# Spreading three tiles, a late norm and a shorter opening in a linear-attention and MLP kernel on one core

## The chip, the cores and the metric

The kernel runs on one core of one Trainium2 chip. The metric is the time of one execution on the device in microseconds (us), the median of several runs. TensorE (PE in the profile; PEld is its weight loads) makes the matrix products, VectorE (DVE), ScalarE (ACT) and GpSimd (POOL) work on their results, SyncE (SP) issues transfers.

## The reference, cut to what matters

```python
kv  = einsum('bhsd,bhse->bhde', k, v)          # 8 batches, 8 heads, 576 rows, 64 columns
out = einsum('bhsd,bhde->bhse', q, kv)
out = out / sqrt(mean(out*out, -1) + 1e-6) * g_norm
x   = out as 4608 tokens x 512                 # heads side by side
h   = x @ w_in                                 # 512 x 2048
g   = max(h, 0) + alpha * min(h, 0)
y   = g @ w_out                                # 2048 x 512
```

The inputs are f32, products are made in f16 and summed in f32.

## The kernel before

The 4608 tokens are worked in nine blocks of 512. A block has 16 units. A unit is one group of four h products (`w_in`, 128 of the 2048 columns), its relu on ScalarE and its `gt` on VectorE; TensorE fills the rest of the unit with y products of finished `gt`s.

```python
def m1_evac(h_ps, w, g):                       # after the four h products of unit g
    nc.scalar.activation(out=m_sb, in_=h_ps, func=Relu, scale=-1.0)
    nc.vector.scalar_tensor_tensor(out=gt, in0=m_sb, scalar=beta[g], in1=h_ps, ...)
```

Attention comes in two forms. Batches 0 and 1 are made with columns of x in PSUM: `step_ot` (product and square), `ssq_mm` (a product that sums squares over a head, then Ln and Exp on ScalarE), `norm` (VectorE). The last 128 columns of batch 1, the "tail", belong to block 2 and go the same way. Batches 2 to 7 are made in tiles of 128 rows, spread over units of the block before: `tile_a` (product, square on ScalarE), `tile_b` (reduce on VectorE), `tile_c` (Ln, Exp, and `rg` on GpSimd), `tile_d` (the row on VectorE, and a transpose by DMA into `xm`, the block's x). Block 2's x is the tail and the first three tiles of batch 2, which are made in block 1.

```python
def tile_d(b, t):
    nc.vector.tensor_mul(out=x, in0=ot_ps, in1=rg)
    nc.sync.dma_start_transpose(out=xm(w)[:, :, c:c+m], in_=x)      # xm(w): all 512 columns of block w

lags = (0, 1, 3) if w == NB_PE else (0, 1, 2)                       # units between a, b+c and d
...
step_tail_ot(0, O1)                  # ahead of block 1
...                                  # in block 1, after unit 1 and unit 3:
            if (w, g) == (1, 1): step_tail_ssq(0, (ps_o, "o0"))
            if (w, g) == (1, 3): tail_norm(0)
            if (w, g) == (1, 2):     # gate: q and k of batch 3 load after q of batch 2 is transposed
                nc.gpsimd.tensor_copy(out=gate, in_=qtms[2][0:1, 0, 0:1]); load(3, "q"); load(3, "k")
            if (w, g) == (1, 11):    # gate: v of batch 3 loads after block 2's x has landed
                nc.gpsimd.tensor_copy(out=gate, in_=xm(2)[0:1, 0, W-1:W]); load(3, "v")
```

A load of q, k or v is two transfers, 320 and 256 KB. The opening (batches 0 and 1) has idle products, `keep_warm(n)`, that are meant to keep the TensorE clock up; block 0's y products fill TensorE while batch 1's attention is made, from about 32 to 50 us.

Of the kernel before, what the change touches and what calls it, by code (L numbers as in the profile page):

```python
# [17 lines left out]
def kernel(  # L18
# [11 lines left out]
    nc = tc.nc  # L30
# [9 lines left out]
    TPW = W // P  # L40
# [4 lines left out]
    NF = D_FF // P  # L45
# [3 lines left out]
    NB_PE = 2  # L49
# [35 lines left out]
    stages, bufs = [], []  # L85
# [4 lines left out]
    def zero_rest(st):  # L90
        nc.vector.memset(st[REM:P, :, TPP, :], 0.0)
# [30 lines left out]
        for nm in ("q", "k"):  # L122
            regroup(b, nm, eng=nc.gpsimd)

    for st in stages:
        for nm in "qkv":
            zero_rest(st[nm])

    ident = const_p.tile([P, P], FP32, name="ident")
    make_identity(nc, ident[:])  # L130
# [17 lines left out]
    nc.vector.memset(eps_t[:], 1e-6)  # L148
    ident16 = const_p.tile([P, P], FP16, name="ident16")
    nc.vector.tensor_copy(out=ident16[:], in_=ident[:])  # L150

    g2col = const_p.tile([P, 1], FP32, name="g2col")
    nc.sync.dma_start(out=g2col[0:64, :], in_=g_norm[:].unsqueeze(1))
# [48 lines left out]
    def keep_warm(n):  # L202
        for i in range(n):
            nc.tensor.matmul(  # L204
                out=warm_ps[:], lhsT=mask16[:], rhs=warm16[:], start=True, stop=True,
            )
# [84 lines left out]
    def ssq_mm(w, j, pool=(ps_o, "o2")):  # L291
        ot_ps, sq = ots.pop((w, j))
        ssq_ps = pool[0].tile([P, W], FP32, name="ssq_ps", tag=pool[1])
        nc.tensor.matmul(out=ssq_ps[:], lhsT=mask16[:], rhs=sq[:], start=True, stop=True)
        rstd = attn_p.tile([P, W], FP32, name="rstd")
        nc.scalar.activation(  # L296
            out=rstd[:], in_=ssq_ps[:], func=AF.Ln, bias=eps_t[:], scale=inv_d,
        )
        nc.scalar.activation(out=rstd[:], in_=rstd[:], func=AF.Exp, bias=0.0, scale=-0.5)  # L299
        ots[w, j] = (ot_ps, rstd)  # L300
# [12 lines left out]
    def half_ot(i, pool, eng=None):  # L313
        ot_ps = pool[0].tile([P, 2, HW], FP32, name="ot_ps", tag=pool[1])
        for u in range(2):
            nc.tensor.matmul(
                out=ot_ps[:, u, :], lhsT=kvs[0, 2 + u],
                rhs=qts[0, 2 + u][:, i * HW : (i + 1) * HW], start=True, stop=True,
            )
        sq = attn_p.tile([P, 2, HW], FP16, name="sq_sb", bufs=4)  # L320
        square(sq, ot_ps, [P, 2, HW], eng)
        ots["half", i] = (ot_ps, sq)
# [23 lines left out]
    def step_tail_ot(i, pool):  # L346
        ot_ps = pool[0].tile([P, JT, TAIL], FP32, name="ot_ps", tag=pool[1])
        for u in range(JT):
            j = i * JT + u
            nc.tensor.matmul(  # L350
                out=ot_ps[:, u, :], lhsT=kvs[NB_PE - 1, j],
                rhs=qts[NB_PE - 1, j][:, S - TAIL : S], start=True, stop=True,
            )
        sq = attn_p.tile([P, JT, TAIL], FP16, name="sq_sb", bufs=4)
        nc.scalar.activation(out=sq[:], in_=ot_ps[:], func=AF.Square)
        ots["tail", i] = (ot_ps, sq)

    def step_tail_ssq(i, pool):
        ot_ps, sq = ots.pop(("tail", i))
        ssq_ps = pool[0].tile([P, JT, TAIL], FP32, name="ssq_ps", tag=pool[1])  # L360
        nc.tensor.matmul(out=ssq_ps[:], lhsT=mask16[:], rhs=sq[:], start=True, stop=True)
        rstd = attn_p.tile([P, JT, TAIL], FP32, name="rstd")
        nc.scalar.activation(
            out=rstd[:], in_=ssq_ps[:], func=AF.Ln, bias=eps_t[:], scale=inv_d,
        )
        nc.scalar.activation(out=rstd[:], in_=rstd[:], func=AF.Exp, bias=0.0, scale=-0.5)
        ots["tail", i] = (ot_ps, rstd)

    def tail_norm(i):
        ot_ps, rstd = ots.pop(("tail", i))  # L370
        nc.vector.scalar_tensor_tensor(
            out=xm(NB_PE)[:, i * JT : (i + 1) * JT, 0:TAIL], in0=ot_ps[:], scalar=g2col[:],
            in1=rstd[:], op0=ALU.mult, op1=ALU.mult,
        )
# [18 lines left out]
    def next_o():  # L393
        n_tile[0] += 1
        return ps_o, f"o{(n_tile[0] - 1) % 3}"
# [48 lines left out]
    def phase_steps(w):  # L444


        if w >= NW:
            return []
        todo = [(b, t) for b in range(NB_PE, min(B, w + 1)) for t in range(NT)
                if (b, t) not in done and b * S + t * P < (w + 1) * W]  # L450
        done.update(todo)
        steps = []

        kv_at = {NB_PE: 3, NB_PE + 1: 6, NB_PE + 2: 2}.get(w, 0)
        n = {NB_PE: 4, NB_PE + 1: 2}.get(w, 0)
        steps += [([], [], []) for i in range(n)]

        lags = (0, 1, 3) if w == NB_PE else (0, 1, 2)
        if w in (NB_PE + 1, NB_PE + 2):
            k = [b for b, t in todo].index(w)  # L460
            todo[k:k] = [None] * (3 if w == NB_PE + 1 else 1)
        for i in range(len(todo) + lags[2]):
            a, b, d = (
                [todo[i - k]] if 0 <= i - k < len(todo) and todo[i - k] else [] for k in lags
            )
            begin = [lambda x=x: tile_b(*x) for x in b] + [lambda x=x: tile_d(*x) for x in d]
            mid = [lambda x=x: tile_c(*x) for x in b]
            end = [lambda x=x: tile_a(*x) for x in a]
            steps.append((begin, mid, end))
        if w < B:  # L470
            steps[kv_at][2 if w == NB_PE else 1].append(lambda: step_kv(w, pool=next_o() if kv_at else (ps_s, "s")))
        return steps
# [91 lines left out]
    )  # L564
    spread_g()
    load_rest()
    keep_warm(4)
    step_kv(0, 0, 2)
    keep_warm(2)
    step_ot(0, 0)  # L570
# [8 lines left out]
    load_batch(2)  # L579
    half_ot(0, (ps_s, "s"))  # L580
    norm(0, 1)
    half_ot(1, (ps_y, "y"), nc.vector)
    first = [ps_h.tile([P, W], FP32, name="h_ps", tag=f"h{g}") for g in range(3)]
    first += [ps_o.tile([P, W], FP32, name="h_ps", tag=f"o{g}") for g in range(2)]
    m1_mm(first[0], 0, 0, (0,))
# [34 lines left out]
    def ahead(g0, g1, tiles=range(TPW)):  # L620
        for g in range(g0, g1):
            for a in tiles:
                y_mm(ys[a], 0, a, g)

    S_POOL = (ps_s, "s")
    O1 = (ps_o, "o1")
# [12 lines left out]
    step_ot(1, 0, H_POOL[0])  # L639
    step_ot(1, 1, O1)  # L640
    step_ot(1, 2, H_POOL[1], nc.vector)
    ahead(8, 9)
    ssq_mm(1, 0, S_POOL)
    ahead(9, 10)
    ssq_mm(1, 1, S_POOL)
    norm(1, 0)
# [10 lines left out]
    y_out(ys[0], 0, 0)  # L657
    ahead(QW, NF, (1,))
    norm(1, 3)
    step_tail_ot(0, O1)  # L660
    ahead(QW, NF, (2,))
    y_out(ys[1], 0, 1, nc.vector)
    y_out(ys[2], 0, 2)
# [8 lines left out]
    AHEAD = NF - 2  # L672
    for w in range(1, NW):
        steps = phase_steps(w + 1)
        for g in range(NF):
            if g == LOAD_G and 4 < w + 2 < B:
                load_batch(w + 2)
            if w == 1:
                parts = [(0, g - NF + AHEAD)] if g >= NF - AHEAD else []
            else:  # L680
                n0 = AHEAD if w == 2 else 0
                n1 = TPW * NF - n0
                parts = [divmod(n0 + i, NF) for i in range(n1 * g // NF, n1 * (g + 1) // NF)]
            begin, mid, end = steps.pop(0) if steps else ([], [], [])
            for f in begin:
                f()
            m1_group(w, g, [H_POOL[1], S_POOL, H_POOL[2], H_POOL[0]][g % 4] if w == 1 else None)
            for f in mid:
                f()
            for a, gg in parts:  # L690
                if gg == 0:
                    pool, tag = ((ps_y, "y"), (ps_s, "s"))[a % 2]
                    y = pool.tile([P, W], FP32, name="y_ps", tag=tag)
                wy = w if w == 1 else w - 1
                y_mm(y, wy, a, gg)
                if gg == NF - 1:
                    y_out(y, wy, a)
            if (w, g) == (1, 1):
                step_tail_ssq(0, (ps_o, "o0"))
            if (w, g) == (1, 3):  # L700
                tail_norm(0)
            for f in end:
                f()
            if (w, g) == (1, 0):
                regroup(2, "k", eng=nc.gpsimd)
            if (w, g) == (1, 2):


                gate = const_p.tile([1, 1], FP16, name="gate")
                nc.gpsimd.tensor_copy(out=gate[:], in_=qtms[2][0:1, 0, 0:1])  # L710
                load(3, "q")
                load(3, "k")
            if (w, g) == (1, 8):
                regroup(3, "q", eng=nc.gpsimd)
            if (w, g) == (1, 11):

                nc.gpsimd.tensor_copy(out=gate[:], in_=xm(2)[0:1, 0, W - 1 : W])
                load(3, "v")
                transpose_q(3)
                regroup(3, "k", eng=nc.gpsimd)  # L720
            for i in {5: (0, 1), 6: (2, 3), 7: (4,), 8: (5,)}.get(g, ()) if w == 2 else ():
                load_part(4, "qkv"[i // 2], i % 2 == 0)
            if w > 1 and g == LOAD_G + 3 + 3 * (w == 2) and w + 2 < B:
                regroup_batch(w + 2)
            if w > 1 and g == NF - 3 and w + 2 < B:
                transpose_q(w + 2)
# [43 lines left out]
```

## Time and profile before

| | before |
|---|---|
| median, range of 4 runs | 293.52 us, 293.33 to 294.04 |
| span of the profiled run | 291.4 us |
| TensorE busy | 96% |
| time between TensorE starts beyond the columns' own time | 7.95 us |
| of it before 21.2 us / 21.2 to 73 us / after | 5.06 / 2.86 / 0.03 |
| first product of blocks 1, 2, 3 | 50.14, 70.89, 98.10 us |

The fourth row counts, for each product, the time to the start of the next less columns/2.4 + 2.5 ns (216 ns for 512 columns). Such time ahead of one product is called a hole below.

### The profile page before, as it was taken

What the parts mean: (1) busy time and instruction counts of PE and PEld (TensorE: products, weight loads), DVE (VectorE), ACT (ScalarE), POOL (GpSimd) and SP (SyncE); (2) the same over time, 40 slices, a digit from 0 to 9 for tenths busy, and PEclk for the clock granted to TensorE, in tenths of its full rate; (3) what the DMA queues carried; (4) which work ended last, traced back from release to release, by engine and by line L of the source; (5) the groups of instructions that cost most, each with busy time, mean ns of one, the idle gap of its engine ahead of it and who ended that gap; (6) DMA issues with size and microseconds to landing.
All of it is one profiled execution on the core that took longest, in us unless ns stands there. A gap on an engine that the chain in (4) does not pass through costs nothing.

```text
span 291.4 us, 4273 instructions
## 1 busy us (share of the span) xinstructions
PE 280.4 (96%) x1547; PEld 137.0 (47%) x1547; DVE 167.5 (57%) x258; ACT 153.6 (53%) x299; POOL 99.1 (34%) x109
## 2 busy tenths in 40 slices
PE   4999999999999999999999999999999999999994
PEld 1444464444454454454445544554445444444443
DVE  4469745687668576448744764488448644444300
ACT  1379349675657565438644754476448544444210
POOL 8822421565358228424733373233003100000000
PEclk9999999999999999999999999999999999999999
DMA  7999999999699916991699179844212311222133
GB/s 91 198 206 205 198 205 198 190 218 148 115 119 213 193 30 107 209 198 31 106 207 205 34 122 207 167 49 90 46 36 56 81 36 41 47 48 47 37 74 72
DMA packets 66197, 35.54 MB, mean 122 GB/s; under 512 B 32753, under 2 KB 61697, under 8 KB 66177
## 3 DMA queue, kind: packets, MB, share of 16 engines
q0 software_dynamic: 29632, 18.35, 45.0%
q1 hardware_dynamic: 36384, 16.80, 28.3%
q8 instruction: 12, 0.20, 0.3%
q10 hardware_dynamic: 160, 0.13, 0.2%
q14 instruction: 9, 0.07, 0.1%
HBM read 36.71 MB, written 9.44 MB: 158 GB/s over the span
## 4 chain that ended last, share of the span: by engine, by line
PE 88%; ACT 3%; DVE 3%; DMA 2%; issue 1%; POOL 1%; DVEq 0%; POOLq 0%
PE h_ps L482 40%; PE y_ps L509 38%; PE kv_ps L245 3%; PE otm_ps L401 2%; DMA qst<-in_q_dram 2%; DVE gt L491 1%; PE yb L509 1%; PE yc L509 1%; PE ya L509 1%; PE yd L509 1%; PE qt_ps L221 1%; ACT m_sb L489 1%; ACT rstd L296 1%; PE ot_ps L278 1%; ACT rstd L299 1%
## 5 line engine op out<-in xcount | busy, mean ns | idle before, releaser
L491 DVE SCALAR_TENSOR_TENSOR gt<-m_sb,beta_sb,h_ps 128x512 f16<-128x512 f32 x144 | 105.6, 744 | 75.8 <-ACT m_sb L489 75.5
L509 PE MATMUL y_ps<-w_out_sb,gt 128*128 128x512 f16 (+1 forms) x528 | 131.3, 373 | 0.8 <-DVE gt L491 0.8
L489 ACT ACTIVATE m_sb<-h_ps 128x512 f32<-128x512 f32 x144 | 85.4, 597 | 85.8 <-PE h_ps L482 84.0
L482 PE MATMUL h_ps<-xm,w_in_sb 128*128 128x512 f16 x448 | 115.0, 379 | 0.0
L509 PEld LDWEIGHTS <-gt 128*128 128x128 f16 x592 | 57.5, 98 | 66.8 <-DVE gt L491 2.7
L482 PEld LDWEIGHTS <-w_in_sb 128*128 128x128 f16 x584 | 55.6, 98 | 60.5 <-issue 1.0
L425 POOL TENSOR_TENSOR rg<-ss,g_all 128x512 f32<-128x512 f32 (+1 forms) x30 | 31.2, 1041 | 80.5 <-ACT ss L423 75.7
L482 PE MATMUL h_ps<-xt,w_in_sb 128*128 128x512 f16 (+1 forms) x136 | 30.8, 366 | 0.5 <-DMA w_in_sb<-in_moe_w_in_dram 0.3
L519 ACT COPY y_sb<-y_ps 128x512 f32<-128x512 f32 (+1 forms) x32 | 18.4, 576 | 15.6 <-PE y_ps L509 15.3
L413 DVE TENSOR_REDUCE ss<-sqm_sb 128x8 f32<-128x512 f32 (+1 forms) x30 | 20.5, 683 | 9.6 <-ACT sqm_sb L407 9.4
L434 DVE TENSOR_TENSOR xrow<-otm_ps,rg 128x512 f16<-128x512 f32 (+1 forms) x30 | 20.5, 682 | 3.6 <-POOL rg L425 3.6
L407 ACT ACTIVATE sqm_sb<-otm_ps 128x512 f32<-128x512 f32 (+1 forms) x30 | 17.7, 590 | 7.2 <-PE otm_ps L401 7.2
L112 POOL COPY ksb<-kst 128x2560 f16<-128x2560 f16 x6 | 13.9, 2324 | 15.7 <-DMA kst<-in_k_dram 15.7
L112 POOL COPY qsb<-qst 128x2560 f16<-128x2560 f16 x5 | 11.6, 2316 | 8.5 <-issue 8.5
L401 PEld LDWEIGHTS <-qtm 128*128 128x128 f16 x120 | 9.2, 98 | 7.9 <-issue 1.1
L401 PE MATMUL otm_ps<-kv_sb,qtm 128*128 128x128 f16 x120 | 11.6, 219 | 0.6 <-DVE kv_sb L249 0.6
L204 PE MATMUL warm_ps<-warm,mask 128*128 128x512 f16 x21 | 7.3, 489 | 4.1 <-DVE eps_t L148 4.1
L245 PEld LDWEIGHTS <-ksb 128*128 128x128 f16 x160 | 9.6, 98 | 2.5 <-issue 0.8
L420 ACT ACTIVATE ss<-ss,eps_t 128x8 f32<-128x8 f32 (+1 forms) x30 | 9.0, 301 | 2.8 <-DVE ss L413 2.6
L245 PE MATMUL kv_ps<-vst,ksb 128*128 128x128 f16 x160 | 10.4, 219 | 0.0
L231 ACT COPY qt_sb<-qt_ps 128x576 f16<-128x576 f16 x4 | 2.4, 638 | 12.4 <-PE qt_ps L221 12.4
L249 DVE TENSOR_TENSOR kv_sb<-kv_ps,mask 128x512 f16<-128x512 f32 (+1 forms) x9 | 5.6, 625 | 5.2 <-PE kv_ps L245 5.2
(76 smaller groups left out, 129.5 us busy)
## 6 DMA issues: line engine op xcount, KB each, us to landing
out_dram<-y_sb SPq DMA_DIRECT2D x70, 128.0 KB, 2.4
qst<-in_q_dram POOLq DMA_DIRECT2D x8, 320.0 KB, 4.8
kst<-in_k_dram POOLq DMA_DIRECT2D x7, 320.0 KB, 8.7
vst<-in_v_dram POOLq DMA_DIRECT2D x7, 320.0 KB, 10.5
qst<-in_q_dram POOLq DMA_DIRECT2D x8, 256.0 KB, 6.3
w_in_sb<-in_moe_w_in_dram POOLq DMA_DIRECT2D x4, 512.0 KB, 10.1
w_out_sb<-in_moe_w_out_dram POOLq DMA_DIRECT2D x4, 512.0 KB, 14.4
kst<-in_k_dram POOLq DMA_DIRECT2D x7, 256.0 KB, 9.5
```

The costliest lines, as they stand in the source:

```text
L112: (eng or nc.vector).tensor_copy(out=bufs[b % NBUF][nm][:, :, h0:h1, :].rearrange("p t h d -> p h t d"), in_=stages[b % NBUF][nm][:, h0:h1],)
L245: nc.tensor.matmul(out=kv_ps[:, j - j0, :], lhsT=ks(t), rhs=vs(t), start=(t == 0), stop=(t == NT - 1),)
L401: nc.tensor.matmul(out=ot_ps[:, 2 * j : 2 * j + 2, :], lhsT=qtms[b][:, t * NPAIR + j, :], rhs=kvs[b, j], start=True, stop=True,)
L407: nc.scalar.activation(out=sq[0:n], in_=ot_ps[0:n], func=AF.Square)
L413: nc.vector.tensor_reduce(out=ss[0:n], in_=sq[0:n], op=ALU.add, axis=mybir.AxisListType.X,)
L425: nc.gpsimd.tensor_tensor(out=rg[0:n], in0=ss[0:n].unsqueeze(2).to_broadcast([n, H, D]), in1=g_all[0:n].unsqueeze(1).to_broadcast([n, H, D ...
L434: nc.vector.tensor_mul(out=x[0:n], in0=ot_ps[0:n], in1=rg[0:n])
L482: nc.tensor.matmul(out=h_ps[:, cols], lhsT=w_in_blk(c, g), rhs=xt_of(w, c)[:, cols], start=(c == 0), stop=(c == NC - 1 and cols.stop == W),)
L489: nc.scalar.activation(out=m_sb[:], in_=h_ps[:], func=AF.Relu, scale=-1.0)
L491: nc.vector.scalar_tensor_tensor(out=gt[:], in0=m_sb[:], scalar=beta_sb[:, g : g + 1], in1=h_ps[:], op0=ALU.mult, op1=ALU.add,)
L509: nc.tensor.matmul(out=y[:], lhsT=gts[w, g][:, a * P : (a + 1) * P], rhs=w_out_blk(g)[:, cols], start=(g == 0), stop=(g == NF - 1),)
L519: nc.scalar.copy(out=y_sb[:, cols], in_=y[:])
```

## The change

Its intent: in block 1, keep VectorE and ScalarE from getting more work in a few units than they can finish; free a bank earlier for the fourth `ot`; start TensorE's useful work sooner.

```diff
 opening
-    for st in stages:                          # memsets of both buffers first
-        for nm in "qkv": zero_rest(st[nm])
+    for nm in "qkv": zero_rest(stages[0][nm])   # the other buffer's come after the constants
...
-    keep_warm(4)
+    keep_warm(2)
...
-    half_ot(1, (ps_y, "y"), nc.vector)          # square by copy and product on VectorE
+    half_ot(1, (ps_y, "y"))                     # square on ScalarE

 batch 1
-    ahead(8, 9)
+    ahead(8, 9, range(2))
     ssq_mm(1, 0, S_POOL)
+    ahead(8, 9, range(2, TPW))
...
-    step_tail_ot(0, O1)

 block 1
-        lags = (0, 1, 3) if w == NB_PE else (0, 1, 2)
+        lags = (0, 1, 4) if w == NB_PE else (0, 1, 2)
+        if w == NB_PE:
+            todo = [x for t in todo for x in (t, None)][:-1]     # a tile every second unit
...
-            if (w, g) == (1, 1): step_tail_ssq(0, (ps_o, "o0"))
-            if (w, g) == (1, 3): tail_norm(0)
+            if (w, g) == (1, 9): step_tail_ot(0, next_o())
+            if (w, g) == (1, 11): step_tail_ssq(0, next_o())
+            if (w, g) == (1, 13): tail_norm(0)
...  (the two pieces of batch 3's work on GpSimd: after unit 9 and 12 instead of 8 and 11)

 block 2: y products per unit
-                parts = [... for i in range(n1 * g // NF, n1 * (g + 1) // NF)]
+                n1, d = TPW * NF - n0, 2 * (w == 2)                # one in the first unit, not three
+                cut = lambda i: max(0, (n1 + d) * i // NF - d)
+                parts = [... for i in range(cut(g), cut(g + 1))]
```

More of the change, by code (lines that the diff above doesn't have):

```diff
@@ L123, in regroup_batch @@
             regroup(b, nm, eng=nc.gpsimd)
-    for st in stages:
-        for nm in "qkv":
-            zero_rest(st[nm])
+    for nm in "qkv":
+        zero_rest(stages[0][nm])
     ident = const_p.tile([P, P], FP32, name="ident")
@@ L150 @@
     nc.vector.tensor_copy(out=ident16[:], in_=ident[:])
+    for nm in "qkv":
+        zero_rest(stages[1][nm])
     g2col = const_p.tile([P, 1], FP32, name="g2col")
@@ L681 @@
                 n0 = AHEAD if w == 2 else 0
-                n1 = TPW * NF - n0
-                parts = [divmod(n0 + i, NF) for i in range(n1 * g // NF, n1 * (g + 1) // NF)]
+                n1, d = TPW * NF - n0, 2 * (w == 2)
+                cut = lambda i: max(0, (n1 + d) * i // NF - d)
+                parts = [divmod(n0 + i, NF) for i in range(cut(g), cut(g + 1))]
             begin, mid, end = steps.pop(0) if steps else ([], [], [])
@@ L697 @@
                     y_out(y, wy, a)
-            if (w, g) == (1, 1):
-                step_tail_ssq(0, (ps_o, "o0"))
-            if (w, g) == (1, 3):
-                tail_norm(0)
             for f in end:
                 f()
+            if (w, g) == (1, 9):
+                step_tail_ot(0, next_o())
+            if (w, g) == (1, 11):
+                step_tail_ssq(0, next_o())
+            if (w, g) == (1, 13):
+                tail_norm(0)
             if (w, g) == (1, 0):
@@ L712 @@
                 load(3, "k")
-            if (w, g) == (1, 8):
+            if (w, g) == (1, 9):
                 regroup(3, "q", eng=nc.gpsimd)
-            if (w, g) == (1, 11):
+            if (w, g) == (1, 12):
                 nc.gpsimd.tensor_copy(out=gate[:], in_=xm(2)[0:1, 0, W - 1 : W])
```

## The prediction

> **What bounds the kernel now.** I read the page first (busy shares, the row of DMA), then the waits of the two TensorE rows, then the chain in order of time for 50 to 73 us, and at each place where TensorE stood still the timeline and the landing of the transfer concerned.
>
> ```profile
> PE 280.4 (96%) x1547; PEld 137.0 (47%) x1547; DVE 167.5 (57%) x258; ACT 153.6 (53%) x299; POOL 99.1 (34%) x109
> DMA  7999999999699916991699179844212311222133
> ```
>
> TensorE is the bound. Its spans overlap (512 columns are shown as 379 ns, yet successive products start 216 ns apart), so I count time lost as start to next start less 216 ns (56 ns for 128 columns). By that count 7.9 us of the 291.4 are lost, all before 73 us: 4.8 before 21 us, the rest in few holes. The transfer row is full until about 45 us. From 73 us on products follow each other without a hole, so time saved earlier counts one for one, unless a transfer then comes late.
>
> The holes of block 1 (the second 512 tokens, 50.1 to 70.9 us), in the chain in order of time:
>
> ```profile
> 54.42 1.41 DVE gt L491 x2
> 55.83 0.66 DVE xm L371
> 56.49 0.61 DVE kv_sb L249
> 57.09 0.14 issue
> 57.23 0.38 PE otm_ps L401 x4
> ...
> 62.45 0.67 DVE xrow L434
> 63.12 0.67 DVE gt L491
> 63.79 0.05 issue
> 63.84 0.39 PE y_ps L509
> ```
>
> Twice the chain leaves TensorE for VectorE. The masked kv stands behind xm (the late norm of batch 1's last columns): the product before started at 56.22, so 57.23 - 56.22 - 0.216 = 0.79 us are lost. Then three tiles in successive units pile up reduces and rows ahead of gt: 0.76 before 63.84, and by the same count 0.165 each before 65.09 and 66.34. The weight row names the same releaser, and kv_sb's as "issue":
>
> ```profile
> PEld L509 <- DVE gt L491: 2.7, 4, 1.1
> PEld L401 <- issue: 1.1, 1, 1.1
> PEld L278 <- DVE xt L305: 0.7, 1, 0.7
> ```
>
> Before block 1 the fourth ot waits for a bank that batch 1's first norm frees; the start of block 2 waits for the last gt:
>
> ```profile
> 44.35 0.38 PE L509 MATMUL yd<-w_out_sb,gt 128*128 128x512 f16 x1
> 44.94 0.39 PE L278 MATMUL ot_ps<-qt_sb,kv_sb 128*128 128x64 f16 x2 [0.21 <-DVE xt L305]
> ...
> 71.75 0.38 PE L509 MATMUL y_ps<-w_out_sb,gt 128*128 128x512 f16 x1
> 72.31 0.60 PE L509 MATMUL y_ps<-w_out_sb,gt 128*128 128x512 f16 x2 [0.18 <-DVE gt L491]
> ```
>
> These are 0.375 and 0.34 us; 0.08 more lies ahead of the ssq at 43.49. Last, where the opening ends for good: the kv of batch 1, and the last part of v that it needs.
>
> ```profile
> 38.48 0.38 PE L509 MATMUL yd<-w_out_sb,gt 128*128 128x512 f16 x1
> 38.77 1.28 PE L245 MATMUL kv_ps<-vst,ksb 128*128 128x128 f16 x20
> ```
>
> The second fence is the view of one tile, narrowed to that transfer's issue: when it was issued, and how long it took to land.
>
> ```profile
> L102 POOL DMA_DIRECT2D vst<-in_v_dram x1: 677/677/677, 25.4 to 25.4; - x1
> DMA to landing us min/median/max: 13.2/13.2/13.2
> ```
>
> 25.4 + 13.2 = 38.6: kv started as soon as v had landed, with TensorE 0.07 us early. This decides what the opening is worth.
>
> **What the Trainium skill says.** "TensorE: Matmul & The Clock Gate", section "Back-to-back issue gap": N/2.4 + 2.5 ns warm, 216 ns for 512 columns; the starts in this trace agree, so 379 ns spans must not be summed. "PSUM — Partial Sum Buffer", section "Engine vs sequencer instructions": VectorE and ScalarE run strictly in order; the trace agrees (kv_sb behind xm above), so moving an instruction in a queue is the whole effect of this change. "DMA: Bandwidth & Descriptors", section "Issuing engines are not separate DMA queues": all share 16 engines; the trace agrees: the transpose of a row issued at 63.15 took 4.8 us to land under batch 3's loads, the one at 66.40 took 2.5 after them.
>
> **The change part by part.**
>
> 1. Opening. Two idle products go (2 x 0.216 = 0.43 us); three memsets of 0.27 us move behind the constants, so warm-up starts 0.8 us earlier, which nothing waits for (q lands at 7.8 us either way). The second half's square moves from VectorE (0.68 + 0.69, ready at 18.76) to ScalarE (0.58, ready about 17.3 by my estimate). But the first slice of w_in lands at 9.0 + 7.5 = 16.5, when the first h product starts now, and the second at 18.98, against 19.05 for its first user. What can go is mainly the 0.34 us hole at 20.6 to 21.2. And then q of batch 1 (landed 35.5, regrouped to 36.41; its transposes start 36.71) and v (38.6) hold TensorE: of anything gained, 0.07 survives. **-0.07.**
>
> 2. ssq of batch 1 two products earlier. ssq 41.90 instead of 42.33, then Ln 0.69, Exp 0.63, norm 0.75 with their gaps follow 0.43 earlier: the norm ends at 44.45 instead of 44.88. The fourth ot needs it at 44.57. Both holes close: **-0.45.**
>
> 3. Tail and tiles in block 1. The tail's four products and ssq (0.22 + 0.22) move into the block, no work is added. I laid out the block by hand, zero at its first product: a unit is 4 x 0.216 = 0.86, from unit 2 on plus one y of 0.216; kv 1.12 after unit 3, tiles 0.22 after 4, 6, 8, tail 0.22 after 9, ssq after 11. ScalarE starts a relu 0.20 after the last product's slot; relu 0.60; gt 0.74; reduce and row 0.69 and 0.68, about 0.07 less apiece back to back. kv ends at 5.00, kv_sb is then first in line and done at 5.88; the first tile starts at 6.08: the 0.79 is gone. gt 4 to 9 end at 7.44, 8.75, 9.90, 11.17, 12.45, 13.73, and the y that need them come at 8.25, 9.55, 10.63, 11.94, 13.24, 14.32: two units of spacing leave 0.6 us or more. The tight end is where the tail's Ln and Exp (1.35 us) hold relu 12 until 16.4: gt 12 ends at 17.78, wanted at 17.78; the tail norm ends at 19.14, wanted by block 2 at 19.13. The third row ends at 16.70, and its transpose with 2.5 us of landing comes at 19.25. So I leave 0.25 us of waiting, of 1.88 lost now: **-1.63.**
>
> 4. Block 2 takes one y instead of three in its first unit: the last y of the first 128 tokens comes 1.08 us later than its gt needs. **-0.34.**
>
> Block 3's first product now waits 0.03 us, counted as gone. Sum: 0.07 + 0.45 + 1.63 + 0.34 + 0.03 = 2.52; 293.48 - 2.52 = 290.96. I add 0.15 because every error in so tight a layout adds a wait: **291.1 us.**
>
> **Rivals.**
> (a) The opening's 0.43 to 0.6 us counts in full: about 290.5. For it: TensorE is the bound on average. Against: the 38.6 landing.
> (b) Block 2 starts on a transfer: the last transpose takes 4.8 us, not 2.5, because batch 3's loads are still in flight. They landed by 67.4; I put the issue at 66.2 of the new run (block 1 starts at 50.14 - 0.07 - 0.45 - 0.22 = 49.4). That costs up to 1 us: 292.
> (c) VectorE still falls behind near the tail, whose norm and ssq now meet the third tile: a wait takes the place of the one removed, 0.5 to 1 us: 291.6 to 292.
> (d) Block 3 gives it all back. Its columns' last transpose landed at 98.05 and its first product started at 98.10: no slack at all. If batch 4's loads (issued 81.0 to 88.6, landed by 96.3) did not move, all gain of parts 2 to 4 would be a wait there: 293.4. Against: GpSimd issues them behind its own work for block 2's tiles, so they follow TensorE's progress. I give this one in ten.
> (e) The warm-up ends at about 7.5, 0.9 us before the transposes, and the clock could rise later; the opening's slack before 38.6 would hide it.
>
> **Range and chances.** All holes after 38 us sum to 2.75, so without (a) the floor is 290.7, with its last 0.4 us about 290.3. (b) and (c) set the upper side at 292.3; (d) lies beyond and is most of the chance left out. Two per cent is 5.9 us, more than twice all holes after 38 us together, and nothing is added to TensorE: faster 0.01, within 2% 0.98, slower 0.01.
>
> **What would show it.** Right: the hole before batch 1's kv, or before its q transposes, grows from 0.07 to about 0.4 us in sum and kv stays at 38.7; no hole at ot (44.5); the waits of TensorE's weight row for gt fall from 2.7 us to below 0.7 and the 1.1 for kv_sb vanishes; block 2's first product moves from 70.9 to about 68.7, and block 3's from 98.1 to about 95.6. Wrong: kv of batch 1 well before 38.6 (a), a wait for xm at the start of block 2 (b) or block 3 (d), or holes on gt around units 10 to 14 (c).

## More of the kernel before

The lines that carry the reading are shown in the prediction. Two more serve as a measure for later: the two stretches from the first product of block 1 to that of block 2, and on to that of block 3. Columns: stretch, its length, and busy time (and instructions) of PE, PEld, DVE, ACT, POOL, then the granted clock, the DMA share and GB/s.

```profile
50.14:70.89 20.75, 19.52 (x113) 9.21 (x111) 15.58 (x24) 13.28 (x29) 10.98 (x12) 1.00 1.18 191
70.89:98.10 27.21, 27.03 (x155) 13.23 (x154) 18.93 (x29) 16.76 (x35) 16.86 (x16) 1.00 1.01 151
```

VectorE is busy 15.6 of 20.75 us in block 1, so it has time enough. What it lacks is the right order.

## The result

| | before | changed |
|---|---|---|
| median | 293.52 us | 291.50 us |
| range of 4 runs each | 293.33 to 294.04 | 291.14 to 291.92 |
| span of the profiled run | 291.4 us | 289.9 us |
| first product of blocks 1, 2, 3 | 50.14, 70.89, 98.10 | 49.59, 69.77, 96.60 |

The ratio is 0.9929, with a 95% interval of 0.9909 to 0.9949. Ratios here are the mean time of one kernel's fast runs over that of the other's of the same rounds, so not quite the ratio of the medians quoted. 2.0 us were gained where 2.4 were predicted. The profiled run is the slowest of its four, so its trace shows 1.5 us of the gain.

The page of the changed kernel, its busy shares and its chain by engine:

```profile
PE 278.7 (96%) x1545; PEld 136.9 (47%) x1545; DVE 166.1 (57%) x256; ACT 154.4 (53%) x300; POOL 99.4 (34%) x109
...
PE 81%; DMA 12%; DVE 2%; ACT 2%; POOL 1%; issue 1%; POOLq 0%; DVEq 0%; ACTq 0%
```

TensorE is busy for the same share. In the second line DMA has 12%, where the page before has 2% (and PE 88%). That is not time lost: by its lines the chain gives 7.6% to q of batch 1 and 3.2% to `w_in`, transfers of the opening at whose landing TensorE now stands waiting, so that their whole flight counts in the chain, and only 1.2% to `xm`. What is lost, the waits of TensorE and of its weight loads from 10 to 100 us say (waiter, released by, us in total, times, longest):

```profile
PE h_ps L485 <- DMA xm<-xrow: 1.0, 1, 1.0
...
PE qt_ps L222 <- DVE qsb L112: 0.6, 1, 0.6
...
PEld L485 <- DMA xm<-xrow: 1.4, 1, 1.4
...
PEld L512 <- DVE gt L494: 0.5, 2, 0.2
```

Weight loads waiting for gt fell from 2.7 us in four waits to 0.5 in two, and no product after 40 us waits for VectorE. In their place stands one wait for a transfer, at the first product of block 2. The chain in order of time (start, us, what) shows it whole:

```profile
65.85 0.35 ACT m_sb L492
66.20 3.44 DMA xm<-xrow
69.63 0.14 issue
69.77 1.02 PE h_ps L485 x4
```

The last row's transpose was issued at 66.20 and landed at 69.63. The last y product of block 1 had started at 68.44, so TensorE was free at 68.44 + 0.216 = 68.66 and stood still for 1.11 us. The same two stretches as before:

```profile
49.59:69.77 20.18, 19.23 (x117) 9.65 (x115) 16.37 (x25) 14.37 (x29) 10.70 (x11) 1.00 1.24 191
69.77:96.60 26.83, 26.83 (x154) 13.40 (x155) 18.17 (x28) 16.23 (x34) 17.70 (x17) 1.00 1.05 157
```

Block 1 became 0.57 us shorter although it took over 0.44 us of products; without the wait it would have been 20.18 - 1.11 = 19.07. Block 2 became 0.38 shorter. Block 1 also starts 0.55 us earlier. Sum: 1.50 us, the gain of the profiled pair.

The opening, in the timeline (start, us, engine, line, operation, and in brackets idle time before it with its releaser):

```profile
35.70 0.38 PE L512 MATMUL yd<-w_out_sb,gt 128*128 128x512 f16 x1
35.79 0.83 DVE L112 COPY qsb<-qst 128x2560 f16<-128x2560 f16 x1 [2.08 <-DMA qst<-in_q_dram]
...
36.67 1.12 PEld L222 LDWEIGHTS <-qsb 128*128 128x128 f16 x20 [1.09 <-DVE qsb L112]
...
38.85 0.24 PEld L246 LDWEIGHTS <-ksb 128*128 128x128 f16 x4 [0.52 <-issue]
```

TensorE came to batch 1's transposes at 35.70 + 0.22 = 35.92, 0.8 us ahead of before, and waited 0.76 us for q and its regrouping, then 0.22 for v. The kv started at 38.88; before, at 38.77. Nothing of the opening survived.

### The profile page after: what moved, and what is told of

Its sections match the earlier page's. It is cut to its first block, busy times and chain, and to the rows that moved or that the text cites. A ratio compares the mean times of both kernels' runs of the same rounds, so it can differ in the third digit from the quotient of the medians.

```text
span 289.9 us, 4268 instructions
## 1 busy us (share of the span) xinstructions
PE 278.7 (96%) x1545; PEld 136.9 (47%) x1545; DVE 166.1 (57%) x256; ACT 154.4 (53%) x300; POOL 99.4 (34%) x109
## 4 chain that ended last, share of the span: by engine, by line
PE 81%; DMA 12%; DVE 2%; ACT 2%; POOL 1%; issue 1%; POOLq 0%; DVEq 0%; ACTq 0%
PE y_ps L512 37%; PE h_ps L485 35%; DMA qst<-in_q_dram 8%; DMA w_in_sb<-in_moe_w_in_dram 3%; PE kv_ps L246 3%; PE otm_ps L402 2%; DMA xm<-xrow 1%; DVE gt L494 1%; ACT m_sb L492 1%; PE yd L512 1%; PE yb L512 1%; PE yc L512 1%; PE ya L512 1%; DVE ss L414 1%; PE qt_ps L222 0%
## 5 line engine op out<-in xcount | busy, mean ns | idle before, releaser
L494 DVE SCALAR_TENSOR_TENSOR gt<-m_sb,beta_sb,h_ps 128x512 f16<-128x512 f32 x144 | 105.8, 744 | 75.7 <-ACT m_sb L492 75.2
L205 PE MATMUL warm_ps<-warm,mask 128*128 128x512 f16 x19 | 6.4, 474 | 3.3 <-DVE eps_t L147 3.3
```

The costliest lines, as they stand in the source:

```text
L494: nc.vector.scalar_tensor_tensor(out=gt[:], in0=m_sb[:], scalar=beta_sb[:, g : g + 1], in1=h_ps[:], op0=ALU.mult, op1=ALU.add,)
```

## The experiments

Twelve runs, on three chips. Each was timed in five rounds against the kernel before; all gave correct results. The changed kernel was not timed again, so a run is set beside it by the ratio to the kernel before, and the traces are single executions.

**1. The opening alone.** The kernel before with the three edits under "opening" in the diff.

> The kernel before with the opening's edits alone (memsets later, two idle products fewer, second half square on ScalarE). My theory: the landing of batch 1's q and v (35.5 and 38.6 us) holds TensorE, so kv of batch 1 still starts at 38.7 and the time stays within 0.15 us of before; the holes before the q transposes and before kv grow to about 1 us in sum. Rival: TensorE time saved in the opening counts, 0.4 to 0.7 us less.

293.99 us against 293.59, ratio 1.0006 (0.9993 to 1.0020): no gain. In its trace the hole ahead of the q transposes is 0.62 us, ahead of kv 0.32, and kv starts at 38.92. This is the theory's picture, and the rival is out: kv starts 0.15 us later than before, not earlier. (0.29 us more were lost where block 3's first product waited for its columns.)

**2. The opposite test.** The changed kernel with more idle work in the opening.

```diff
-    keep_warm(2)
+    keep_warm(6)
     step_kv(0, 0, 2)
```

> The changed kernel with six idle products instead of two in the opening: 4 x 0.216 = 0.86 us of TensorE time added where the change took 0.43 away. Theory: batch 1's q and v hold TensorE for about 0.97 us (0.76 and 0.22 in the changed kernel); the added time is taken from these holes, kv of batch 1 still starts at 38.7 to 38.9 and the time stays within 0.2 us of the changed kernel. Rival: opening time counts, 0.5 to 0.9 us more.

291.70 us, 0.9932 of before, against 0.9929 for the changed kernel: 0.86 us of added TensorE time cost nothing that can be measured. The time alone would not show this, because the wait at block 2 takes up lateness too: TensorE came there 0.21 us later than in the changed kernel and still waited 0.35 us. The start of kv does show it. In the timeline the holes are filled, and kv is merely 0.2 us later:

```profile
38.87 0.38 PE L512 MATMUL yd<-w_out_sb,gt 128*128 128x512 f16 x1
39.09 0.33 PE L246 MATMUL kv_ps<-vst,ksb 128*128 128x128 f16 x3
```

Taking 0.43 us out of the opening and putting 0.86 in came out alike. The landing of batch 1's q and v bounds this stretch.

**3. The earlier ssq alone.** The kernel before with the two `ahead` lines of the diff.

> The kernel before with batch 1's first ssq product two products earlier, nothing else. Theory: the holes of 0.375 and 0.08 us at 43 to 45 us close and nothing else moves until block 1; 0.3 to 0.45 us less than before in block 1's start. At the end less may be left if block 2 or block 3 then starts on a transfer: 0 to 0.45 us less. Rival: the hole only moves to a later ssq, no gain at block 1's start.

293.11 us, ratio 0.9983 (0.9971 to 0.9994). The two holes at 43 to 45 us are gone, and the first products of blocks 1, 2 and 3 come 0.51, 0.51 and 0.53 us earlier than before. Alone, this part is worth its 0.45 us.

**4. Block 1's part alone.** The kernel before with the edits under "block 1" and "block 2" and the tail's removal.

> The kernel before with the block 1 part alone (tiles two units apart, tail late, one y in block 2's first unit). Theory: the 1.9 us of holes on VectorE in block 1 and the 0.34 at its end go, a wait for the transposes into xm of about 0.7 us at block 2's first product comes (it lands at about 69.6 whatever TensorE does); 1.5 us less than before, 291.9 to 292.1. Rival (the three parts simply add): 0.45 us behind the whole change, at 291.95, with no smaller wait for xm than in the whole change, 1.1 us. The wait in the trace tells the two apart.

291.41 us, ratio 0.9927 (0.9915 to 0.9940): all of the whole change's gain without the other two parts, and half a microsecond better than I had expected (the profiled run, 292.07, is the slowest of its five). In its profile xm lands at 69.75, where the whole change has 69.63, and the wait is the smaller one, 0.87 us. The earlier ssq brought TensorE to block 2 at 68.66 instead of 69.02, and it waited that much longer. So the gains do not add: the transfer sets the start of block 2.

**5. Tiles apart, tail as before,** and **6. tail late, tiles as before.** The two halves of block 1's part.

> The kernel before with the tiles of block 1 two units apart (and the two loads that follow them one unit later), tail and block 2 as before. Theory: the three holes on gt in block 1 (0.76 + 0.165 + 0.165 = 1.09 us) go, the 0.79 before the first tile stays; the last row and its transpose come about 1.3 us later than before (issue near 67.7), so block 2 starts on the transposes, with a wait for xm up to 0.7 us. Time 0.4 to 1.1 us below before. Rival: the holes come from the tail, not from the tiles; they stay and the time is that of before.

292.59 us, ratio 0.9957 (0.9941 to 0.9973). The holes on gt are gone, the hole of 0.79 us before the first tile is still there. The wait for xm is 0.20 us: its last transpose was issued at 67.66 and landed at 70.04.

> The kernel before with the tail's norm late in block 1, tiles in successive units as before. Theory: the 0.79 us before the first tile goes, most of the 1.09 us on gt stays or grows a little; rows and transposes as early as before, so no wait for xm at block 2 (its start near 70.1 is past their landing at 68.5 to 69). The 0.34 us at the start of block 2 stays. Time 0.6 to 0.9 us below before, 292.7. Rival: TensorE, 0.8 us ahead, meets the same VectorE backlog and the hole on gt grows by as much, time of before.

292.84 us, ratio 0.9970 (0.9955 to 0.9985). The 0.79 us are gone. The holes on gt, 0.76 + 0.165 + 0.165 before, are now 0.98 and 0.12, here the larger one:

```profile
62.88 0.39 PE L509 MATMUL y_ps<-w_out_sb,gt 128*128 128x512 f16 x1 [0.81 <-DVE gt L491]
```

So the holes on gt come from the tiles in successive units, and the one before the first tile from the tail's norm, as predicted. What neither theory had: block 3's first product waits 0.34 us for its columns.

**7. Rows one unit earlier.** Is the transpose late because the spacing makes its row late?

```diff
-        lags = (0, 1, 4) if w == NB_PE else (0, 1, 2)
+        lags = (0, 1, 3) if w == NB_PE else (0, 1, 2)
```

> The changed kernel with each tile's last step three units after its first instead of four, so the rows and their transposes are issued one unit (1.08 us) earlier. Theory: the transposes into xm land about 0.3 to 1.1 us after batch 3's last load whenever they are issued; landing stays at 69.2 to 69.7, the wait at block 2's first product stays at 0.7 us or more (or part of it turns into waits for gt in block 1), and the time is within 0.4 us of the changed kernel. Rival: the spacing itself made the third row late (issued at 66.2 plus a fixed landing time); then landing moves to 68.6 and the time falls by 1 us to 290.5.

292.17 us, ratio 0.9949 (0.9934 to 0.9965): slower than the changed kernel if anything, by 0.67 us in the medians, where at most 0.4 was expected. The last transpose was issued at 65.4, 0.8 us earlier, and took 4.4 us instead of 3.4 (the view of xm narrowed to it: issue, then time to landing):

```profile
L440 SPq DMA_TRANSPOSE xm<-xrow x1: 1874/1874/1874, 65.4 to 65.4; - x1
...
DMA to landing us min/median/max: 4.4/4.4/4.4
```

It landed at 69.81, and TensorE, earlier too, waited 1.45 us. The issue is not what makes it late. A warning on reading: in this run the timeline puts the product's wait down to VectorE, and only the weight load ahead of it names the transfer. The gt that is named had no bearing on it.

```profile
69.91 0.13 PEld L485 LDWEIGHTS <-w_in_sb 128*128 128x128 f16 x2 [1.75 <-DMA xm<-xrow]
69.94 0.38 PE L485 MATMUL h_ps<-xm,w_in_sb 128*128 128x512 f16 x1 [1.29 <-DVE gt L494]
```

**8. Less load in flight.** The second part of batch 3's k goes behind the gate, with v.

```diff
                 load(3, "q")
-                load(3, "k")
+                load_part(3, "k", True)
...
+                load_part(3, "k", False)
                 load(3, "v")
```

> The changed kernel, with the second part of batch 3's k (256 KB) loaded behind the gate that waits for xm, instead of before it. Theory: the transposes into xm land late because batch 3's loads (the last at 68.6 us) share the DMA engines with them; with the last load out of the way the third transpose lands about 2.5 us after its issue at 66.2, at 68.7 to 68.9, the 1.1 us wait at block 2's first product falls to under 0.3, and the time falls by 0.8 to 1.1 us against the changed kernel, to about 290.6. Rival: the transposes are late by their own issue or among themselves: landing stays at 69.6 and the time at 291.5. A third way: v of batch 3 then lands too late for its kv (about 78.8 us) and the gain is given back there.

The transposes did what the theory said: issued at 66.38, landed at 68.80, 2.4 us later, and the wait at block 2 is 0.09 us. The time did not: 292.94 us, ratio 0.9977 (0.9965 to 0.9989), slower than the changed kernel. The third way came, and worse than written down. The kv of batch 3 waited 0.52 us for v, and block 3's first product 1.63 us for its columns. GpSimd now regroups k when it lands at 75.7; behind that stand its work for block 2's tiles and batch 4's loads (the first issued at 80.07 instead of 79.24), which end at 97.5 instead of 94.5. The waits from 20 to 100 us, in part:

```profile
PE h_ps L485 <- DMA xm<-xrow: 1.5, 1, 1.5
PE kv_ps L246 <- DMA vst<-in_v_dram: 0.4, 1, 0.4
```

The first of these is block 3's. That is rival (d) of the prediction, set off by an edit that delayed a load.

**9. Stores out of the way.** The output stores of block 0's third and fourth 128 tokens (four of eight, 0.5 MB) are issued by SyncE behind block 1's row transposes.

```diff
 def y_out(..., later=None):
-            queues[i // REM].dma_start(out=rows[t][:, cols], in_=y_sb[i : i + REM, cols])
+            def store(...): queues[i // REM].dma_start(...)          # the same transfer
+            store() if later is None else later.append(store)
...
-    y_out(ys[2], 0, 2)
+    y_out(ys[2], 0, 2, later=late_stores)       # and ys[3] likewise
...
             if (w, g) == (1, 12):
+                for f in late_stores: f()
```

> The changed kernel, with the output stores of the third and fourth 128 tokens (4 of 8, 0.5 MB) issued behind the row transposes of block 1 instead of ahead of them. Theory: these stores share the DMA engines with batch 3's q and k and with the transposes; without them the last k load lands 1.5 to 2.5 us earlier (about 66.5 instead of 68.6), the third transpose at 68.6 to 68.9, the wait for xm falls from 1.1 to under 0.3 us, v of batch 3 still lands before its kv at 78.8, and block 3 finds its columns. Time 0.8 to 1.1 us below the changed kernel, about 290.6. Rival: the stores cost the loads nothing, landing stays at 69.6 and the time at 291.5; or v of batch 3, now beside the stores, lands later than 78.8 and takes the gain.

291.21 us, ratio 0.9916 (0.9901 to 0.9931); about 290.6 was expected, and the interval overlaps with the changed kernel's. Batch 3's last k part landed at 65.85 instead of 68.64, the last transpose at 68.55, and block 2 starts 0.05 us after TensorE is free (the view of xm narrowed to that one issue, then the timeline):

```profile
L440 SPq DMA_TRANSPOSE xm<-xrow x1: 1190/1190/1190, 66.2 to 66.2; - x1
...
DMA to landing us min/median/max: 2.4/2.4/2.4
```

```profile
68.69 1.02 PE L485 MATMUL h_ps<-xm,w_in_sb 128*128 128x512 f16 x4
```

Half of this was given back: the stores now run beside v of batch 3, which landed at 79.28 instead of 77.91, and its kv waited 0.57 us:

```profile
79.41 0.77 PE L246 MATMUL kv_ps<-vst,ksb 128*128 128x128 f16 x11 [0.41 <-DMA vst<-in_v_dram]
```

**10. Stores late, without the earlier ssq.**

> The one before this (stores late) without the earlier ssq product. Theory: the whole change and its block 1 part alone came out equal because TensorE's 0.45 us from the earlier ssq was waited away for xm; with that wait gone the 0.45 us shows: this run is 0.3 to 0.5 us slower than the one with the earlier ssq, about 291.0, with its holes of 0.375 and 0.08 us at 43 to 45 us and the wait for xm near zero. Rival: the ssq is worth nothing in the presence of the other parts; both runs agree within 0.1.

291.73 us, 0.52 above the run with it, and the ranges (291.34 to 291.96 against 290.99 to 291.32) do not meet. But the profiled pair doesn't show it: there the 0.45 us came back in the wait for v (0.15 us here, 0.57 with the earlier ssq), and block 3 starts at 96.07 and 96.09. The medians agree with the theory; I don't call it shown.

**11. Three y products in block 2's first unit again,** otherwise the changed kernel.

> The changed kernel, but with three y products in block 2's first unit as before. Theory: in the changed kernel block 2's first product waits for xm (1.1 us in its trace), and the gt that these y products need are done by then, so that the hole of 0.34 us cannot come back: within 0.15 us of the changed kernel, no hole on gt in block 2's first unit. Rival (my prediction): this part is worth 0.34 us by itself, and the hole is back at block 2's first unit, 0.3 us slower.

291.93 us, ratio 0.9933 (0.9916 to 0.9951); the intervals overlap widely with the changed kernel's. As the theory had it, there is no hole on gt in block 2's first unit: TensorE had waited 0.94 us for xm just before, and the gt were done. But block 2 is 27.22 us long, not 26.83: block 3's first product waited 0.39 us for its columns. SyncE's queue tells why. First the run without the new distribution, then the changed kernel:

```profile
90.77 1.18 SPq L530 DMA_DIRECT2D out_dram<-y_sb  x2
92.04 2.50 SPq L440 DMA_TRANSPOSE xm<-xrow  x2
```

```profile
89.51 4.34 SPq L440 DMA_TRANSPOSE xm<-xrow  x3
93.95 1.18 SPq L530 DMA_DIRECT2D out_dram<-y_sb  x2
```

With fewer y products early in block 2, a finished 128 tokens come one unit later, and their store falls behind the last transposes of block 3's columns instead of ahead of them. These land at 95.24 instead of 96.70. The last load ahead of them is 0.73 us later in this run too (95.19 against 94.46). But in the seven traces with the new distribution (run 8, with its late k, left aside) the transpose in question landed 0.77 to 0.88 us after that load, in the six without it 1.35 to 1.74 us. So this part seems to have its worth (about 0.4 us in the traces) by another way than the one I predicted; no run moves the store alone.

**12. A version meant to beat both.** Late stores, and batch 3's kv after the y products of its unit.

```diff
-            steps[kv_at][2 if w == NB_PE else 1].append(...)
+            steps[kv_at][2 if w in (NB_PE, NB_PE + 1) else 1].append(...)
```

> The changed kernel with the late stores (third and fourth 128 tokens), and batch 3's kv after the y products of its unit instead of before them (0.65 us later). Theory: with late stores the wait for xm was gone, but v of batch 3 landed at 79.3 and its kv waited 0.57 us; three y products ahead of it cover that wait. Block 3 then starts about 0.5 us earlier than with late stores alone (95.6 instead of 96.1): about 290.7 to 290.9, below both kernels. Rival: block 3's columns (its last transpose lands later by the shifted tiles) take it back: 291.2.

290.81 us (290.70 to 290.99), ratio 0.9900 (0.9884 to 0.9917). The range lies below the changed kernel's (291.14 to 291.92) and ends where that of late stores alone begins (290.99). They were run at other times. As the intervals of the ratios overlap (the changed kernel's is 0.9909 to 0.9949), the traces carry the claim. The same two stretches in this kernel:

```profile
49.50:68.62 19.12, 19.12 (x116) 9.68 (x115) 15.39 (x24) 13.85 (x29) 10.64 (x11) 1.00 1.14 165
68.62:95.45 26.83, 26.83 (x155) 13.38 (x155) 19.23 (x29) 16.64 (x35) 17.72 (x17) 1.00 1.23 184
```

In both, TensorE's busy time is the length of the stretch. Here the prediction's hand-made layout of block 1, with block 2 wanted at 19.13, is what happens.

The runs side by side; all times from the traces. "k" is the landing of batch 3's last k part ahead of the gate, "free" the end of TensorE's last slot in block 1.

| run | k landed | last transpose issued | landed | took | TensorE free | hole at block 2 |
|---|---|---|---|---|---|---|
| before | 67.43 | 66.40 | 68.90 | 2.5 | 70.89 | 0 |
| changed | 68.64 | 66.20 | 69.63 | 3.4 | 68.66 | 1.11 |
| block 1 alone | 68.51 | 66.56 | 69.75 | 3.2 | 69.02 | 0.87 |
| tiles apart alone | 67.46 | 67.66 | 70.04 | 2.4 | 69.98 | 0.20 |
| tail late alone | 66.92 | 64.87 | 69.81 | 4.9 | 70.15 | 0 |
| rows earlier | 69.14 | 65.37 | 69.81 | 4.4 | 68.49 | 1.45 |
| more idle products | 67.92 | 66.41 | 69.08 | 2.7 | 68.87 | 0.35 |
| three y again | 67.87 | 66.12 | 69.39 | 3.3 | 68.58 | 0.94 |
| half of k late | 66.45 | 66.38 | 68.80 | 2.4 | 68.85 | 0.09 |
| stores late | 65.85 | 66.17 | 68.55 | 2.4 | 68.64 | 0.05 |
| stores late, kv later | 66.19 | 66.10 | 68.48 | 2.4 | 68.56 | 0.06 |

A transpose issued after the loads have landed, or up to 1.0 us before, took 2.4 to 2.5 us. Issued earlier than that, it landed 0.7 to 1.5 us after the last load, however early it was issued. The tail alone is an exception that no run explains: 2.9 us after the last load.

What counts, by the traces, is the loads issued ahead of the transpose. In the changed kernel one was issued at 80.03 and landed at 86.65: 0.87 us after batch 4's q (issued 79.95, landed 85.78), and before its k, which was issued at 80.62 and landed at 89.15. In all traces together, of 115 transposes that were issued between 48 and 95.5 us with such loads in flight, 114 landed after the last of these loads or at most 0.25 us before it.

The landing of k itself moves by over 1 us between runs with the same stores (67.9 to 69.1), and part of the changed kernel's spread may be that: it has 0.8 us between its fastest and slowest run, the three kernels with late stores 0.3, 0.6 and 0.3.

## Why the prediction was right

The time lies within the stated range, 0.4 us above the point. Two of the signs named for "right" failed, though: block 2's first product came at 69.77, not at about 68.7, and block 3's at 96.60, not 95.6. By its own steps:

1. *Opening, -0.07.* Right. The holes before q and kv grew to 0.97 us in sum, more than the "about 0.4" that I named as a sign, because w_in also landed 0.5 us earlier in this run (16.0 instead of 16.5) and let the opening run further ahead. v landed 0.1 us later, so that kv started at 38.88.
2. *The earlier ssq, -0.45.* Right as a part (run 3; in the changed kernel both holes are gone), but in the whole change it was waited away at block 2 (run 4).
3. *Block 1, -1.63.* Here is the term that was mis-sized: "its transpose with 2.5 us of landing comes at 19.25. So I leave 0.25 us of waiting". The rest of the layout held: issue at 66.20 (predicted 66.2), block 2 wanted at 19.07 after the block's start (19.13), no product waiting for gt or kv_sb. But the landing took 3.4 us, not 2.5, and the waiting was 1.11, not 0.25. I had taken the 2.5 from the kernel before, and had read that transpose as one "after" the loads. It wasn't: k of batch 3 landed at 67.43, 1.0 us after that issue; now it landed 2.4 us after it. Why k itself lands later is not isolated by a run. Among the ten kernels with the same loads and stores, the five whose first row transpose was issued before 62 us (61.7 to 60.5) have k at 67.9 to 69.1, the five after it (62.2 to 63.3) at 66.9 to 67.6: the transposes may slow the loads as the loads delay them. Runs 8 and 9 show the reverse: with less in flight the landing is 2.4 us.
4. *Block 2's first unit, -0.34.* The hole went, the amount is right (27.21 to 26.83 us), the reason is not: in the whole change the wait for xm would have covered the hole, and the part earns its 0.4 us by the order of a store and two transposes in SyncE's queue, as far as run 11 shows. That the amount fits is luck.

Of the rivals, (a) is refuted by run 1, and the start of kv in run 2 agrees; (b) came true and is nearly the whole error of the profiled run (0.86 of 0.9 us; the runs near the median were not traced); (c) did not happen; (d) did not happen in the changed kernel, but in run 8 it took away more than that edit had gained, and in runs 1, 6 and 11 block 3 gave back 0.29 to 0.39 us. (e), the clock, got no run of its own, but the traces speak against it. The idle products start 427 ns apart at first; in the changed kernel the step falls to 217 ns at 6.49 us and the q transposes from 8.13 on follow each other at 56 ns, and in the kernel before the step is still 427 ns at 7.44, and 56 ns in the transposes from 8.53. The faster pace came earlier, not later.

In sum: from block 1's start to block 2's I predicted 20.75 to shrink to about 19.3 (49.4 to 68.7) and got 20.18 in the profiled run, the slowest of the four. The other stretches came out within 0.2 us of the prediction.

## What to carry to other kernels

Here TensorE was the bound, its holes were small, and behind most of them another wait stood next in line. So before counting a gain, read when the next transfer lands, and how far ahead of it TensorE will then be. A landing time read in one profile holds only for the traffic of that profile; if the change moves the issue among other transfers, take the landing of the loads issued ahead of it as the floor. And when parts of a change are timed alone, look for the one wait that they all run into: here one part alone gave all the gain, the others fed the wait, and moving 0.5 MB of stores released it, though half of the gain then went into a wait for v until one product group was moved too.

## What the Trainium skill lacked or had wrong

- "DMA: Bandwidth & Descriptors", section "Issuing engines are not separate DMA queues", says that transfers of different engines interleave. It doesn't say how a small DMA transpose fares among large loads: here 2.4 us from issue to landing when the loads were out of the way, 2.5 to 4.9 us for the last of three with loads issued ahead of it still in flight, and 7.5 us for the first of them in the changed kernel (issued 61.36, landed 68.81, 0.17 us after the last load).
- The same page, section "DMA Transpose (X-bar)", gives no time from issue to landing for such a transpose (its section "Latency and other measured facts" has only a bandwidth, 261 GB/s on one kernel); 2.4 us (128 rows of 512, f16, SBUF to SBUF) is this case's number.
- "TensorE: Matmul & The Clock Gate", section "Back-to-back issue gap", gives about 131 ns per 512-column product as the sustained figure of a stream of weight loads and products. Here each product has its own weight load, and the starts of 512-column products are 216 ns apart from 73 us to the end; the page's formula for an isolated product fits, the 131 ns don't.
